# Two attentions on one core: images that hold each part once, key loads a slot ahead, small steps placed later

## The chip, the cores and the metric

The kernel runs on one core of a Trainium2 chip. The metric is the device time of one execution in microseconds, as the median of several runs. TensorE (PE in the profile) multiplies, VectorE (DVE) and ScalarE (ACT) work element by element and read TensorE's results from PSUM, GpSimd (POOL) works on SBUF only, and SyncE (SP) does nothing but send DMAs. Each engine runs its own instructions strictly in the order of the program; engines wait for one another, and for DMAs, by semaphores.

## The reference

```
x = A_x                                     # 2048 x 512, 32 heads of 16
g = sigmoid((x * gate_w).sum(-1))
A: q, k, v = x@wq, x@wk, x@wv, cut in 4 segments of 512 tokens; per segment
     a_dot = softmax(q k^T / 4 + causal mask) v
     a_mem = phi(q) M / (phi(q) z + 1e-6)          # M, z: sums over the segments before
     o = sigmoid(beta) * a_mem + (1 - sigmoid(beta)) * a_dot
   a = o @ wo
B: q, k, v = x @ wqkv;  b = softmax(q k^T / 4) v @ wob     # all 2048 keys
out = g * a + (1 - g) * b
```

A's `wq` and `wk` are scaled by 200, so the scores are large: each softmax needs its true row maximum, and queries and keys need more than one float32r pass. Each is therefore split in a high and a low part (`hi` = rounded to float32r, `lo` = the rest), and a score is hi·hi + hi·lo + lo·hi in one matmul of 48 contraction rows: 16 for each product. Two more rows, 48 and 49 of each half, hold minus the row maximum in two parts, so that the matmul of the scores subtracts it.

## The kernel before

**The projections** (the first 410 us or so) compute q, k and v of A and B from the transposed x, split q and k, and write them to HBM as *images* `QKD[kd, w, g]`: for each head rows of 2048 tokens. `kd` is A or B, `w` is 0 for queries and 1 for keys, `g` a group of eight heads. In A's images each part stands once (`lo`, `hi` for queries, `hi`, `lo` for keys); B's have three parts (`hi`, `lo`, `hi` and `hi`, `hi`, `lo`), and the third is written by a DMA on GpSimd's queue (L295). The same phase computes A's memory term and stores it to HBM (`OM`).

**The loop** has 32 slots, k = 0 to 31. A unit is four heads and 512 queries. Slot k handles unit 32+k, which is B's unit (`ub`), with 16 key tiles in 32 steps n = 0 to 31, and then unit k of A (`ua`) in five steps, n = 32 to 36. Two steps make one `it` (`it = n // 2`; the last step, 36, has it = 18). A step sends, in this order on TensorE: the transposed scores of two heads (`t_group`, L503), whose exponential ScalarE takes into `raw` (L509); the tasks that the plan puts there; and the product with V for an earlier step (`pv`, L525), summed in the PSUM bank `PVB`.

**Row maxima** are found a slot early, by tasks in the plan. `s_b` (L449) computes the scores of 128 queries against 512 keys for two heads into one of two PSUM buffers `sbk`, and VectorE reduces them (L451). B's unit 33+k has 32 such tasks: twelve in steps 20 to 31 of slot k-1, and twenty in steps 1 to 19 of slot k, step 1 having two. A's six tasks (`s_a`) are in steps 32 to 36 and step 0. At it = 10 `m_chain` (L460 to L470) makes minus the maximum in two parts, and after step 24 `m_rows` sends it into the query tile.

**The end of a unit.** `fin_copy` copies `PVB` to SBUF (L532 on VectorE for A, in step 0 of the next slot; L534 on ScalarE for B, in step 33) and writes it to HBM (L536). `fin_load` reads back the sums' row in another shape (L544) and the outputs (L542). `fin_rec` takes the reciprocal on VectorE (L549, then L553 for B or L551 for A) and writes it (L555). `fin_bc` reads it back, spread over the partitions (L561). Every second slot `fin_norm` multiplies on GpSimd (L565), fetches the memory term for B (L568), and for A adds the two branches (L570). `out_split` splits a block of 128 tokens for the output matmul: ScalarE rounds (L584), GpSimd subtracts (L585). `out_mm` (L591) multiplies it with `wo` and `wob` in step 20 of slots 9 and later. `beside(k, it)` says at which `it` each of these is put into the program.

**Loads.** `load_q` and `load_kb` (both L370) read query tiles and B's keys, all 2048 tokens of four heads. B's key buffers are three (`KB`, named `kb` and `xh` in the profile, since two of them are former x tiles), its query tiles three. In slot k after it = 2 the keys of index k+2 are loaded; the row maxima of that index begin at step 20 of the same slot. `load_q(ua+1)` and `load_ka` follow after it = 6, B's values (`load_vb`) and `wo` after it = 8.

**The order** is written out by hand: nothing reorders it. All these DMAs go through SP's one queue in program order; a DMA that has to wait for data holds all that follow. In the trace a key load of A waits 26 times (39.6 us in all) for the landing of a `d<-rd`, the eighth DMA before it in the queue, though it uses nothing of it.

Of the kernel before, what the change touches and what calls it, by code (L numbers as in the profile page):

```python
# [7 lines left out]
FT = mybir.dt.float32  # L8
# [10 lines left out]
E = 16  # L19
SEQ = 2048  # L20
DM = 512
C = 512
NC4 = SEQ // C
NT = SEQ // 128
# [3 lines left out]
S_FIRST = 10  # L28
S_LAST = 10
# [4 lines left out]
def gated_mix_kernel(ctx, tc, x, wq, wk, wv, wo, beta, wqkv, wob, gate_w, out):  # L34
    nc = tc.nc
# [6 lines left out]
    D = ctx.enter_context(tc.tile_pool(name="dram", bufs=1, space=DRAM))  # L42
# [52 lines left out]
    def misc():  # L95
        return bank(mode["misc"])

    QKD = {}
    for kd in "AB":
        for w in range(2):  # L100
            for g in range(4):
                QKD[kd, w, g] = D.tile([8, (3 if kd == "B" else 2) * E + 2 * (w == 0), SEQ], FT, name=f"d{kd}{w}{g}")
    VD = {kd: D.tile([SEQ, 4, 8, E + 1], FT, name=f"vd{kd}") for kd in "AB"}
    GD = D.tile([SEQ], FT, name="gd")
    OM = {}
# [168 lines left out]
    def qk_job(ws, kd, g, w, c):  # L274
        b = misc()
        n = 0
        for xi, wi in TERMS:
            for k in range(4):
                nc.tensor.matmul(b, WS[ws][w][wi][:, k, :], (XH, XL)[xi][c][:, k, :], start=n == 0, stop=n == 11)  # L279
                n += 1  # L280
        st = X.tile([128, 2, C], FR, name="st", bufs=4)
        phi = kd == "A" and (c > 0 if w == 0 else c < NC4 - 1)
        if phi:
            ph = PHI[g, w, c] = X.tile([128, C], FT, name=f"phi{w}")
            nc.vector.tensor_scalar(ph, b, 0.0, None, op0=OP.min)
        nc.scalar.activation(st[:, 0], b, AF.Copy)
        if phi:
            nc.scalar.activation(ph, ph, AF.Exp)
        nc.vector.tensor_tensor(st[:, 1], b, st[:, 0], op=OP.subtract)  # L289
        if phi:  # L290
            nc.vector.scalar_tensor_tensor(ph, b, 0.0, ph, op0=OP.max, op1=OP.add)
        img = QKD[kd, w, g][:, :, c * C:(c + 1) * C]
        for n, a in enumerate(((0, 1, 0), (0, 0, 1))[w] if kd == "B" else ((1, 0), (0, 1))[w]):
            eng = nc.gpsimd if n == 2 else nc.sync
            eng.dma_start(img[:, E * n:E * n + E], st[:, a].bitcast(FT))  # L295
        if w == 0 and c == 0:
            nc.sync.dma_start(QKD[kd, w, g][:, (3 if kd == "B" else 2) * E:].rearrange("h r (n t) -> h r n t", t=64),
                              aux[:, 1, None, :].to_broadcast([E, 2 * NT, 64]))


# [61 lines left out]
    def load_qk(dst, kd, w, qd, c):  # L362
        img = QKD[kd, w, qd // 2]
        v = img.rearrange("(q p j) r t -> q j r p t", q=2, p=2)
        cs = slice(c * C, (c + 1) * C) if c is not None else slice(0, SEQ)


        for d0, r0, n in ((0, 0, img.shape[1]),) if kd == "B" else ((0, 0, 16), (16, 0, 32)) if w else ((0, 0, 32), (32, 16, 18)):
            for j in range(2):
                nc.sync.dma_start(dst.bitcast(FT)[64 * j + d0:64 * j + d0 + n], v[qd % 2, j, r0:r0 + n, :, cs])  # L370

# [4 lines left out]
    def q_of(u):  # L376
        return QA[u % 2] if u < 32 else QB[u % 3]
# [4 lines left out]
    def load_q(u):  # L382
        kd, qd, c = UN[u]
        load_qk(q_of(u), kd, 0, qd, c)
# [5 lines left out]
    def load_kb(k, c=None):  # L390
        dst = KB[k % 3] if c is None else KB[k % 3][:, :, c * C:(c + 1) * C]
        load_qk(dst, "B", 1, k % 8, c)
# [6 lines left out]
    def load_vb(g):  # L399
        v_src(VB[g % 2], "B", g % 4, None)  # L400
# [145 lines left out]
    def fin_rec(u):  # L546
        kd, qd, c = UN[u]
        r = AT.pop(("r", u))
        nc.vector.reciprocal(r, r)  # L549
        if kd == "A":  # L550
            nc.vector.scalar_tensor_tensor(r, r, nq[:, qd:qd + 1], grow[:, 0, c], op0=OP.mult, op1=OP.mult)  # L551
        else:
            nc.vector.tensor_tensor(r, r, grow[:, 1, c], op=OP.mult)  # L553
        AT["rd", u] = D.tile([128, E], FT, name=f"rd{u}")
        nc.sync.dma_start(AT["rd", u], r)  # L555
# [7 lines left out]
    def fin_norm(kd, g, c):  # L563
        o, d = AT["o"][c % 2][:, g, int(kd == "B")], AT["d"][int(kd == "B")]
        nc.gpsimd.tensor_tensor(o, o, d, op=OP.mult)  # L565
        if kd == "B":
            if c:
                nc.sync.dma_start(d, OM[g, c])  # L568
        elif c:
            nc.gpsimd.tensor_tensor(o, o, AT["d"][1], op=OP.add)  # L570
# [12 lines left out]
    def out_split(c, t):  # L583
        nc.scalar.activation(AT["oh"], o_cols(c, t), AF.Copy)  # L584
        nc.gpsimd.tensor_tensor(AT["ol"], o_cols(c, t), AT["oh"], op=OP.subtract)  # L585
# [19 lines left out]
    def tail_split(t, gs, a, eng=None):  # L605
        oh, ol = [x[:, gs, a] for x in tail_ops(t)]
        o = o_cols(3, t)[:, gs, a]
        if eng:
            nc.scalar.copy(oh, o)
        else:  # L610
            nc.vector.tensor_copy(oh, o)
        (eng or nc.vector).tensor_tensor(ol, o, oh, op=OP.subtract)
# [20 lines left out]
    def todo(fn, *a):  # L633
        return lambda: fn(*a)
# [86 lines left out]
    for blk in range(16):  # L721
        g, c = divmod(blk, 4)
# [11 lines left out]
        n = blk + 1 + (c == 2)  # L734
# [90 lines left out]
    NG = 2 * NT + 5  # L825
# [34 lines left out]

    def beside(k, it):

        for f, it0, u in ((fin_load, NT + 1, 32 + k), (fin_rec, 1, 31 + k), (fin_bc, 2, 31 + k),
                          (fin_load, 1, k - 1), (fin_rec, 4, k - 1), (fin_bc, 5, k - 1)):
            if it == it0 and (k or it0 > NT):
                f(u)
        c, j = divmod(k - 1, 8)
        if k and j % 2:
            for kd, it0 in (("B", 4), ("A", 12)):
                if it == it0:  # L870
                    fin_norm(kd, j // 2, c)
        if k >= 8 and k % 2 == 0 and it == 14:
            out_split(k // 8 - 1, k // 2 % 4)
        if (k, it) == (31, 4):
            grest = AT["grest"] = AT["o"][0][64:, 0, 0]
            nc.sync.dma_start(grest, GD[3 * C:].rearrange("(o t) -> o t", o=1).to_broadcast([64, C]))
        if (k, it) == (31, 9):
            grest = AT["grest"]
            nc.vector.tensor_scalar(grest, grest, nh[64:, 3:4], None, op0=OP.mult)
        if (k, it) == (31, NT + 2):  # L880
            fin_rec(63)
        if k == 31 and it == 8:
            o = AT["o"][1][:64, 3, 0]
            nc.gpsimd.tensor_tensor(o, o, AT["d"][0][:64], op=OP.mult)
        if k == 31 and it < 8 and it % 2 == 0:
            for a in range(2):
                tail_split(it // 2, slice(0, 3), a)
# [9 lines left out]
    for k in range(31):  # L897
        if k:
            spread([todo(s_b, 33 + k, *t) for t in (sorted(ST_B, key=lambda t: t[2]) if k == 1 else ST_B)],
                   [(k - 1, n) for n in range(2 * S_FIRST, 2 * NT)] + [(k, n) for n in [1] + list(range(1, 2 * S_LAST))])  # L900
        else:
            spread(st33[EARLY:], sorted([(0, n) for n in range(2 * S_LAST)] + [(0, 2 * n) for n in range(4)]))
        for n, t in enumerate(ST_A):
            plan.setdefault((k, 2 * NT + n) if n < 5 else (k + 1, 0), []).append(todo(s_a, k + 1, *t))

    for k in range(32):
        ua, ub = k, 32 + k
        banks = T3 + [SBK[0][:, n] for n in range(2)] * (k == 31)
        for n in range(NG):
            it = n // 2 if n < NG - 1 else NT + 2  # L910
            t_group(*(ub, n) if n < 2 * NT else (ua, n - 2 * NT), banks)
            for f in plan.get((k, n), []) + ex[k][0].get(n, []):
                f()
            pvs(k, n)
            for f in ex[k][1].get(n, []):
                f()
            if n % 2 == 0 and n < NG - 1:
                continue
            beside(k, it)
            if it == S_LAST:  # L920
                m_chain(k + 1)
            if it == 4 and not k:
                late()
            if it == (2 if k else 4) and k < 30:
                load_q(ub + 2)
                for c in (None,) if k else range(NC4):
                    load_kb(k + 2, c)
            if it == 6 and k < 31:
                load_q(ua + 1)
                load_ka(ua + 1)  # L930
                if (ua + 1) % 2 == 0:
                    load_va(ua + 1)
            if it == 8:
                if k % 2 == 0 and k < 30:
                    load_vb(k // 2 + 1)
                if 1 <= k <= 4:
                    load_wo(k - 1)
# [16 lines left out]
    for t in range(4):  # L954
        d = den[:, t * 128:(t + 1) * 128]
# [37 lines left out]
```

## Time and profile before

| | us |
|---|---|
| median of 3 runs | 2071.38 |
| lowest, highest | 2065.68, 2074.39 |
| the profiled execution | 2075.72 |
| its span, first to last instruction | 2073.9 |
| granted TensorE clock, mean | 0.988 |

The profile is of one execution. Its rows give a start in us from the span's start, a duration, an engine, a line of the kernel and what is written from what; a bracket behind a row is the engine's idle time before it and what ended that. The names of the buffers stand without their numbers.

### The profile page before, as it was taken

Reading aid. Unit: us, or ns where it says so; the run is one execution under the profiler, and the core shown is the slowest. Engines: PE = TensorE matmul, PEld = TensorE weight load, DVE = VectorE, ACT = ScalarE, POOL = GpSimd, SP = SyncE. Lnnn points to the kernel's source line nnn. Section 1 sums busy time; section 2 is a strip of 40 time slices with the busy share of each in tenths; the row PEclk is TensorE's granted clock in tenths of the full one; section 3 lists DMA queues with packets and bytes.
Section 4 is the critical chain, followed back from the end, with each engine's and each line's share of the span. In section 5 each row is a group of like instructions: output and inputs, shape, how many; then the busy total and the mean of one; then the engine's idle time right before and its main releaser. Section 6 shows DMA issues by size and latency. Waiting matters only on the chain.

```text
span 2073.9 us, 43532 instructions
## 1 busy us (share of the span) xinstructions
PE 1977.6 (95%) x17517; PEld 958.7 (46%) x17517; DVE 1633.2 (79%) x1825; ACT 1432.9 (69%) x2703; POOL 276.1 (13%) x506
## 2 busy tenths in 40 slices
PE   7999898899999999999999999999999999999988
PEld 5777676533344343444444444444444444344434
DVE  6134564599999999898989898989888888888832
ACT  3232232388888888878787778787878777777783
POOL 2300010011111001111111111111111111101111
PEclk9999999899999999999999999999999999999999
DMA  6766566654544444343434443444444443444201
GB/s 209 178 175 189 176 194 172 185 125 107 119 100 108 94 108 101 82 108 82 108 82 109 82 108 82 105 85 102 89 94 95 88 103 79 100 87 98 60 30 52
DMA packets 165173, 230.88 MB, mean 111 GB/s; under 512 B 39644, under 2 KB 89836, under 8 KB 159212
## 3 DMA queue, kind: packets, MB, share of 16 engines
q1 hardware_dynamic: 157420, 211.69, 42.3%
q0 software_dynamic: 7552, 16.41, 3.5%
q8 instruction: 138, 2.26, 0.5%
q14 instruction: 63, 0.52, 0.1%
HBM read 148.21 MB, written 76.55 MB: 108 GB/s over the span
## 4 chain that ended last, share of the span: by engine, by line
PE 71%; DVE 10%; DMA 10%; ACT 4%; issue 2%; SPq 2%; POOL 0%; ACTq 0%; DVEq 0%; POOLq 0%
PE pvb L525 25%; PE tb L503 13%; PE sbk L449 9%; DVE mxb L451 7%; PE mb L503 6%; DMA xh<-dB 3%; ACT raw L509 2%; PE tb L591 2%; PE sbk L428 2%; PE tb L279 2%; DMA dA<-st 2%; DMA kb<-dB 1%; PE mb L279 1%; PE sbk L431 1%; PE mb L591 1%
## 5 line engine op out<-in xcount | busy, mean ns | idle before, releaser
L451 DVE TENSOR_REDUCE mxb<-sbk 128x2 f32<-128x1024 f32 x1024 | 1204.2, 1218 | 67.7 <-PE sbk L449 64.4
L509 ACT ACTIVATE raw<-tb 128x512 f32<-128x512 f32 x1557 | 885.8, 597 | 191.7 <-PE tb L503 93.2
L525 PE MATMUL pvb<-raw,vb 128*17 128x256 f32 (+1 forms) x8072 | 639.5, 389 | 0.0
L509 ACT ACTIVATE raw<-mb 128x512 f32<-128x512 f32 x780 | 465.6, 597 | 87.5 <-PE tb L503 61.1
L503 PE MATMUL tb<-qb,xh 64*128 64x512 f32 x880 | 333.6, 494 | 1.5 <-ACT raw L509 0.8
L449 PE MATMUL sbk<-xh,qb 64*128 64x512 f32 x1344 | 279.3, 402 | 28.3 <-DVE mxb L451 15.0
L525 PEld LDWEIGHTS pvb<-raw,vb 128*17 128x17 f32 x8072 | 134.4, 95 | 334.5 <-issue 327.5
L503 PE MATMUL mb<-qb,xh 64*128 64x512 f32 x437 | 215.9, 494 | 1.2 <-ACT raw L509 0.8
L512 POOL TENSOR_SCALAR_AFFINE_SELECT raw<-raw 128x256 f32<-128x256 f32 (+1 forms) x320 | 115.3, 361 | 748.0 <-ACT raw L509 739.9
L503 PEld LDWEIGHTS tb<-qb,xh 64*128 64x128 f32 x880 | 125.5, 183 | 189.6 <-issue 100.1
L503 PE MATMUL tb<-qb,kb 64*128 64x512 f32 x463 | 176.2, 496 | 2.6 <-DMA qb<-mr 1.1
L435 DVE TENSOR_REDUCE mx<-sbk 128x2 f32<-128x768 f32 (+1 forms) x128 | 139.8, 1092 | 44.2 <-PE sbk L431 35.3
L449 PE MATMUL sbk<-kb,qb 64*128 64x512 f32 x704 | 148.9, 409 | 13.3 <-DVE mxb L451 11.7
L449 PEld LDWEIGHTS sbk<-xh,qb 64*128 64x128 f32 x1344 | 135.3, 186 | 46.6 <-DVE mxb L451 32.1
L503 PEld LDWEIGHTS mb<-qb,xh 64*128 64x128 f32 x437 | 80.0, 183 | 90.0 <-issue 49.3
L503 PE MATMUL mb<-qb,kb 64*128 64x512 f32 x241 | 118.7, 492 | 0.7 <-DVE st L289 0.7
L503 PEld LDWEIGHTS tb<-qb,kb 64*128 64x128 f32 x463 | 65.9, 183 | 101.3 <-issue 50.7
L525 PE MATMUL pvb<-raw,va 128*17 128x256 f32 (+2 forms) x1280 | 94.8, 384 | 4.2 <-ACT pvs L534 0.8
L565 POOL TENSOR_TENSOR o<-o,d 128x512 f32<-128x512 f32 x31 | 39.8, 1282 | 410.8 <-DMA d<-rd 365.6
L437 DVE TENSOR_REDUCE mx<-sbk 128x4 f32<-128x1024 f32 x64 | 61.4, 960 | 37.6 <-PE sbk L431 37.6
L428 PE MATMUL sbk<-ka,qa 64*128 64x256 f32 (+3 forms) x512 | 85.9, 344 | 0.0
L449 PEld LDWEIGHTS sbk<-kb,qb 64*128 64x128 f32 x704 | 70.5, 186 | 30.2 <-DVE mxb L451 19.2
(266 smaller groups left out, 1866.4 us busy)
## 6 DMA issues: line engine op xcount, KB each, us to landing
xh<-dB SPq DMA_DIRECT2D x38, 768.0 KB
vb<-vdB SPq DMA_DIRECT2D x16, 1088.0 KB
kb<-dB SPq DMA_DIRECT2D x22, 768.0 KB
dB<-st SPq DMA_DIRECT2D x64, 256.0 KB
dA<-st SPq DMA_DIRECT2D x64, 256.0 KB
pd<-pvs SPq DMA_DIRECT2D x64, 256.0 KB
qb<-dB SPq DMA_DIRECT2D x64, 200.0 KB
dB<-st POOLq DMA_DIRECT2D x32, 256.0 KB, 7.3
```

The source lines that it names most:

```text
L279: nc.tensor.matmul(b, WS[ws][w][wi][:, k, :], (XH, XL)[xi][c][:, k, :], start=n == 0, stop=n == 11)
L428: nc.tensor.matmul(b[:, j, c0:c0 + n], q_of(u)[r, p, i * 128:(i + 1) * 128], k_of(u, p)[r, :n], start=True, stop=False)
L435: nc.vector.tensor_reduce(m[:, :, p, i], b[:, :, :n], axis=AX.X, op=OP.max)
L437: nc.vector.tensor_reduce(m[:, :, :, i], b.rearrange("q j (p k) -> q j p k", p=2)[:, :, :, :n], axis=AX.X, op=OP.max)
L449: nc.tensor.matmul(b[:, j], q_of(u)[r, p, i * 128:(i + 1) * 128], k_of(u, p)[r, kc * C:(kc + 1) * C], start=True, stop=True)
L451: nc.vector.tensor_reduce(MXB[u][:, :, p, i, kc], b, axis=AX.X, op=OP.max)
L503: nc.tensor.matmul(bs[j][:, c0:c0 + w], k_of(u, h // 2)[r, 128 * it:128 * it + 128], q_of(u)[r, h // 2, q0:], start=True, stop=True)
L509: nc.scalar.activation(pt, bs[j], AF.Exp, scale=SCALE)
L512: nc.gpsimd.affine_select(out=m, in_=m, pattern=[[1, 128]] if n < 2 else [[0, 2], [1, 128]], compare_op=OP.is_ge, fill=0.0, base=0, channe ...
L525: nc.tensor.matmul(PVB[32 * h:32 * h + E + 1, q0 + lo:q0 + hi], vt[:, it, 4 * q + h, :], pt[:, lo:hi], start=it == 0 and lo == 0, stop=it ...
L565: nc.gpsimd.tensor_tensor(o, o, d, op=OP.mult)
L591: nc.tensor.matmul(b, (AT["oh"], AT["ol"])[oi][:, g, a], (AT["wh"], AT["wl"])[wi][:, g, a], start=n == 0, stop=n == 11)
```

## The change

- B's images have two parts like A's. The third DMA of each of B's query and key jobs, on GpSimd's queue, is gone. `load_qk` reads both kinds as A's were read before: queries in pieces of 32 and 18 rows, keys in pieces of 16 and 32 rows, each for two halves of the partitions, so four DMAs in place of two.
- B's queries and keys of the slot after next are loaded at it = 16 (`NT`), the step after `fin_copy` of B, instead of at it = 2 one slot later. Slot 0 still loads index 2 in four chunks.
- `fin_rec` and `fin_bc` move from it = 1 and 2 to 5 and 6 for B, and from 4 and 5 to 6 and 7 for A. `fin_norm` moves from 4 to 9 for B and from 12 to 13 for A, `out_split` from 14 to 18, the loads of B's values and of `wo` from 8 to 9.
- Of the two maximum tasks in step 1 one goes to step 36 of the slot before.

```diff
-                QKD[kd, w, g] = D.tile([8, (3 if kd == "B" else 2) * E + 2 * (w == 0), SEQ], FT, name=f"d{kd}{w}{g}")
+                QKD[kd, w, g] = D.tile([8, 2 * E + 2 * (w == 0), SEQ], FT, name=f"d{kd}{w}{g}")
...
-        for n, a in enumerate(((0, 1, 0), (0, 0, 1))[w] if kd == "B" else ((1, 0), (0, 1))[w]):
-            eng = nc.gpsimd if n == 2 else nc.sync
-            eng.dma_start(img[:, E * n:E * n + E], st[:, a].bitcast(FT))
+        for a in range(2):
+            r = E * (a if w else 1 - a)
+            nc.sync.dma_start(img[:, r:r + E], st[:, a].bitcast(FT))
...
-        for d0, r0, n in ((0, 0, img.shape[1]),) if kd == "B" else ((0, 0, 16), (16, 0, 32)) if w else ((0, 0, 32), (32, 16, 18)):
+        for d0, r0, n in ((0, 0, 16), (16, 0, 32)) if w else ((0, 0, 32), (32, 16, 18)):
...
-        for f, it0, u in ((fin_load, NT + 1, 32 + k), (fin_rec, 1, 31 + k), (fin_bc, 2, 31 + k),
-                          (fin_load, 1, k - 1), (fin_rec, 4, k - 1), (fin_bc, 5, k - 1)):
+        for f, it0, u in ((fin_load, NT + 1, 32 + k), (fin_rec, 5, 31 + k), (fin_bc, 6, 31 + k),
+                          (fin_load, 1, k - 1), (fin_rec, 6, k - 1), (fin_bc, 7, k - 1)):
...
-            for kd, it0 in (("B", 4), ("A", 12)):
+            for kd, it0 in (("B", 9), ("A", 13)):
...
-        if k >= 8 and k % 2 == 0 and it == 14:
+        if k >= 8 and k % 2 == 0 and it == NT + 2:
             out_split(k // 8 - 1, k // 2 % 4)
...
-        if k == 31 and it == 8:
+        if k == 31 and it == 13:
             o = AT["o"][1][:64, 3, 0]
             nc.gpsimd.tensor_tensor(o, o, AT["d"][0][:64], op=OP.mult)
...
-                   [(k - 1, n) for n in range(2 * S_FIRST, 2 * NT)] + [(k, n) for n in [1] + list(range(1, 2 * S_LAST))])
+                   [(k - 1, n) for n in list(range(2 * S_FIRST, 2 * NT)) + [NG - 1]] + [(k, n) for n in range(1, 2 * S_LAST)])
...
-            if it == (2 if k else 4) and k < 30:
+            if it == 4 and not k:
                 load_q(ub + 2)
-                for c in (None,) if k else range(NC4):
-                    load_kb(k + 2, c)
+                for c in range(NC4):
+                    load_kb(2, c)
+            if it == NT and k < 29:
+                load_q(ub + 3)
+                load_kb(k + 3)
...
-            if it == 8:
+            if it == 9:
                 if k % 2 == 0 and k < 30:
                     load_vb(k // 2 + 1)
```

More of the change, by code (lines that the diff above doesn't have):

```diff
@@ L292, in qk_job @@
         img = QKD[kd, w, g][:, :, c * C:(c + 1) * C]
-        for n, a in enumerate(((0, 1, 0), (0, 0, 1))[w] if kd == "B" else ((1, 0), (0, 1))[w]):
-            eng = nc.gpsimd if n == 2 else nc.sync
-            eng.dma_start(img[:, E * n:E * n + E], st[:, a].bitcast(FT))
+        for a in range(2):
+            r = E * (a if w else 1 - a)
+            nc.sync.dma_start(img[:, r:r + E], st[:, a].bitcast(FT))
         if w == 0 and c == 0:
-            nc.sync.dma_start(QKD[kd, w, g][:, (3 if kd == "B" else 2) * E:].rearrange("h r (n t) -> h r n t", t=64),
+            nc.sync.dma_start(QKD[kd, w, g][:, 2 * E:].rearrange("h r (n t) -> h r n t", t=64),
                               aux[:, 1, None, :].to_broadcast([E, 2 * NT, 64]))
```

## The prediction

> **What bounds the kernel now.** I read the page first, then the busy time of single slots, then one quiet slot row by row. A slot runs from the first score matmul of B's step 0 to the next one.
>
> ```profile
> span 2073.9 us, 43532 instructions
> PE 1977.6 (95%) x17517; PEld 958.7 (46%) x17517; DVE 1633.2 (79%) x1825; ACT 1432.9 (69%) x2703; POOL 276.1 (13%) x506
> ```
>
> TensorE is busy for 95% of the span, so a loss must show as a longer slot. In the next view (columns: stretch, length, then busy time of each engine) the first line is the projections, the second a quiet slot, 23. The sums are of the eleven odd slots 9 to 29, the six even ones 10 to 20 and the four even ones 22 to 28.
>
> ```profile
> 0.00:412.00 412.00, 364.38 (x1699) 277.55 (x1700) 195.30 (x324) 121.52 (x251) 55.27 (x102) 0.95 0.65 185
> 1572.79:1623.83 51.04, 50.54 (x508) 21.61 (x504) 45.64 (x48) 41.27 (x77) 3.60 (x11) 1.00 0.39 83
> sum 564.95, PE 558.66 PEld 238.98 DVE 502.29 ACT 453.44 POOL 39.81; mean PE 50.79 PEld 21.73 DVE 45.66 ACT 41.22 POOL 3.62
> sum 317.15, PE 307.76 PEld 128.87 DVE 285.47 ACT 248.47 POOL 58.97; mean PE 51.29 PEld 21.48 DVE 47.58 ACT 41.41 POOL 9.83
> sum 216.38, PE 205.78 PEld 85.79 DVE 190.71 ACT 165.78 POOL 39.44; mean PE 51.45 PEld 21.45 DVE 47.68 ACT 41.44 POOL 9.86
> ```
>
> Quiet is 51.04 us; odd slots average 51.36, early even ones 52.86, late even ones 54.10. All even slots have about 2 us more VectorE time and 6 us more GpSimd time. Why VectorE's time counts shows in the quiet slot, which starts at 1572.79:
>
> ```profile
> 1575.00 4.61 DVE L451 TENSOR_REDUCE mxb<-sbk 128x2 f32<-128x1024 f32 x4
> ...
> 1586.96 0.23 DVE L551 SCALAR_TENSOR_TENSOR rec<-rec,nq,grow 128x16 f32<-128x16 f32 x1
> 1587.11 13.08 DVE L451 TENSOR_REDUCE mxb<-sbk 128x2 f32<-128x1024 f32 x11
> 1603.10 1.23 DVE L451 TENSOR_REDUCE mxb<-sbk 128x2 f32<-128x1024 f32 x1 [2.91 <-PE sbk L449]
> ...
> 1604.48 0.18 DVE L468 TENSOR_SCALAR mhi<-mx 128x32 fp32r<-128x32 f32 x1
> ```
>
> From 1575.0 VectorE runs 21 row maxima and two reciprocal pairs without a gap, 1.15 us a maximum where it has a backlog (4.61 / 4) and 1.19 over the last eleven; only the output matmuls (2.91 us) let it idle. TensorE can be two maxima ahead (two `sbk` buffers), so anything added here is soon paid by TensorE. The backlog comes from step 1, which holds two maximum tasks:
>
> ```profile
> 1575.44 0.50 PE L503 MATMUL mb<-qb,xh 64*128 64x512 f32 x1
> 1576.27 0.50 PE L449 MATMUL sbk<-kb,qb 64*128 64x512 f32 x2 [0.33 <-DVE mxb L451]
> ```
>
> In even slots GpSimd's products meet VectorE's small SBUF operations (timeline of slot 26, which starts at 1728.70, GpSimd's rows and VectorE's):
>
> ```profile
> 1761.70 1.28 POOL L565 TENSOR_TENSOR o<-o,d 128x512 f32<-128x512 f32 x1 [16.99 <-DMA ka<-dA]
> 1763.07 1.31 POOL L570 TENSOR_TENSOR o<-o,d 128x512 f32<-128x512 f32 x1
> ...
> 1761.74 1.28 DVE L468 TENSOR_SCALAR mhi<-mx 128x32 fp32r<-128x32 f32 x1
> ...
> 1763.15 1.27 DVE L470 SCALAR_TENSOR_TENSOR m<-mx,mhi 128x32 f32<-128x32 f32 x1
> ```
>
> The groups over the loop, with busy us and mean ns behind the bar:
>
> ```profile
> L551 DVE SCALAR_TENSOR_TENSOR rec<-rec,nq,grow 128x16 f32<-128x16 f32 x31 | 14.4, 465 | 1.1
> L470 DVE SCALAR_TENSOR_TENSOR m<-mx,mhi 128x32 f32<-128x32 f32 x32 | 12.4, 388 | 0.0
> L468 DVE TENSOR_SCALAR mhi<-mx 128x32 fp32r<-128x32 f32 x32 | 11.2, 349 | 1.1
> ```
>
> Each ends with the GpSimd operation it met: 1.28 us for 0.18. Over the loop that is (465-233) x 31 = 7.2 us in L551 and, with L468's quiet 0.18 for both, (388-180) x 32 = 6.7 in L470 and (349-180) x 32 = 5.4 in L468. The products are late because SP's queue stands behind the key load (SP's timeline, same slot):
>
> ```profile
> 1735.92 0.33 SPq L555 DMA_DIRECT2D rd<-rec  x1
> ...
> 1737.91 0.51 SPq L561 DMA_DIRECT2D d<-rd  x1
> 1738.47 0.87 SPq L370 DMA_DIRECT2D qb<-dB  x2
> 1739.39 0.81 SPq L370 DMA_DIRECT2D xh<-dB  x2
> 1743.14 0.34 SPq L555 DMA_DIRECT2D rd<-rec  x1
> ...
> 1755.67 0.53 SPq L561 DMA_DIRECT2D d<-rd  x1
> 1756.26 1.67 SPq L370 DMA_DIRECT2D qa<-dA  x4
> 1757.97 3.98 SPq L370 DMA_DIRECT2D ka<-dA  x4
> ...
> 1779.62 0.33 SPq L536 DMA_DIRECT2D pd<-pvs  x1
> ```
>
> The same load in the chain that ended last, and in TensorE's waits over the loop (total, times, longest):
>
> ```profile
> 1739.78 15.63 DMA xh<-dB
> ```
> ```profile
> PE sbk L449 <- DMA xh<-dB: 2.4, 3, 1.0
> ```
>
> A's reciprocals, sent at 1743.14, land only with the keys (15.63 us), so A's broadcast leaves at 1755.67 and its product starts at 1761.70, beside the maximum chain. The keys themselves are late in some slots; TensorE waits for them directly.
>
> **The change, part by part** (gains against the profiled execution, 2075.7 us: the span of 2073.9 and 1.8 around it).
>
> *Keys a slot ahead.* Every late key wait goes: the cover is now 24 steps instead of 15. Price: 4 x (54.10 - 52.86) + 11 x (51.36 - 51.04) = 8.5 us above; below, the 2.4 us of the row. I take 7, nearer the slots than the waits, since a wait also leaves VectorE idle.
>
> *B's reciprocal pair after step 11, A's after 13.* Now B's product, started by its broadcast, meets A's pair. Later B's product can start 2 us (1735.92 to 1737.91) and a broadcast's 5 us (row below) behind B's pair, at about +23 from the slot's start, and A's pair is done by +18.6 (below). L551 meets nothing: 7.2 us, less what the two buffers hide; I take 6 (0 to 7.2).
>
> *The maximum chain.* A broadcast takes 5.0 us from its issue to the product that waits for it, in slot 30, which loads no keys; a reciprocal row takes 3.75 from its issue to the reciprocal that waits (last slot; SP's rows and the waiting engine's):
>
> ```profile
> 1957.20 0.53 SPq L561 DMA_DIRECT2D d<-rd  x1
> ...
> 1962.20 1.28 POOL L565 TENSOR_TENSOR o<-o,d 128x512 f32<-128x512 f32 x1 [6.46 <-DMA d<-rd]
> ...
> 1997.36 0.51 SPq L544 DMA_DIRECT2D rec<-pd  x1
> ...
> 2001.11 0.25 DVE L549 RECIPROCAL rec<-rec 128x16 f32<-128x16 f32 x1 [2.92 <-DMA rec<-pd]
> ```
>
> From a slot's start: A's old pair ends at 1587.1 - 1572.8 = 14.3; four steps of 1.19 later, less the 0.3 saved at step 2 (next part), is 18.8. Its reciprocals are in HBM 2 us later, but now A's queries and keys (eight DMAs, 1.7 + 4.0 us by the rows) are issued ahead of its broadcast: 24 to 24.6, landing 5.0 later, product and sum (2.6 us) from 29 or 29.6 to 31.6 or 32.2. L468 stands at 1604.48 - 1572.79 = 31.7, then 0.3 earlier. So the end of the sum grazes it, 0.2 to 0.8 us in eleven slots instead of 1.1: of the 12.1 us in L468 and L470 I take back 7 (0 to 12.1). In slots 1 to 8, which have no output matmuls, the chain comes 2.9 us sooner and can now be hit; also `wo`'s GpSimd copies arrive earlier. I charge 2 us (0 to 5, four hits of 1.28).
>
> *One maximum task behind A.* The task's own matmuls cost as much in either step. What goes is the 0.33 of idle before step 2's maximum, and with it the backlog through which each reciprocal pair (about 0.4 us) bites later; against it, step 2's scores may wait for a bank anyway. I take 0.3 x 30 slots = 9 us; bounds 0 and, with a second hold of the same size, 0.6 x 30 = 18.
>
> *The split for the output at the slot's end.* ScalarE's 1.06 us goes from the stretch in which every step has two exponentials to the seam, where steps are longer. GpSimd's 2.38 us then lies beside the PVB copy L532 (one line's durations, min/median/max; the group of L585 with its mean).
>
> ```profile
> L584 ACT ACTIVATE oh<-o x12: 1057/1059/1059, 831.6 to 1981.3; 128x1024 fp32r<-128x1024 f32 x12
> L451 DVE TENSOR_REDUCE mxb<-sbk x64: 1207/1216/1227, 1679.6 to 1775.6; 128x2 f32<-128x1024 f32 x64
> L585 POOL TENSOR_TENSOR ol<-o,oh 128x1024 fp32r<-128x1024 f32 x12 | 28.6, 2380 | 129.2 <-ACT oh L584 129.2
> ```
>
> L451 reads PSUM and holds 1207 to 1227 ns through slot 26's products, so I let L532, a PSUM reader too, run free: gain 2 us, bounds 4 and, if it were held 1 us in 12 slots, -12. [...]
>
> *Images with each part once.* These go from the projections (the page's DMA issues: count, size, median us to landing):
>
> ```profile
> dB<-st POOLq DMA_DIRECT2D x32, 256.0 KB, 7.3
> ```
>
> They are 8.4 MB of 185 GB/s x 412 us = 76 MB. TensorE idles 412 - 364 = 48 us there, partly for DMAs; a ninth of half of it is 3 us (-3 to 8; below zero because the first key chunks now take four DMAs each). In a slot SP issues four DMAs more, 4 x 0.43 us; SP waits for landings for most of it, so nothing, and 1.7 us before the bound rows if that cover were gone.
>
> *What is queued behind the early keys.* Keys and queries now leave right after B's sums, 4.0 us before a slot's start (1779.62 against 1783.60) and 0.3 more with the moved task. A's sums are written at about +2.5, behind the keys on the same queue; SP waits for that, then asks for the reciprocal row. Keys: last issue at -4.3 + 8 x 0.4 = -1.1, less than 15.6 to land since no broadcast is ahead of them; I take +10.5 (9 to 13). B's read-backs lie between, an estimated 2 us: sums written +12.5, row asked +13.1, and 2001.11 - 1997.36 = 3.75 to come: +16.9. VectorE wants it at 18.8 - 0.4 = +18.4. Margin 1.5, spread about as large: I charge 0.1 x 29 = 3 us (0 to 38).
>
> Sum: 7 + 6 + 7 - 2 + 9 + 2 + 3 - 3 = 29; 2075.7 - 29 = 2046.7. The median of the runs, 2071.4, is 4.3 below the profiled execution, so a median could come out at 2042; I name 2045, between the two.
>
> **Rivals.** *1. Order is not time.* GpSimd's products are moved in the program, but nothing holds them to a step: they start when the broadcast lands. If it lands 1 us later than reckoned, product and sum sit on the chain as now: 7 us less, 2052. For: eight DMAs now stand before A's broadcast. Against: the key load no longer does.
>
> *2. The sums come late* (the other side). The keys' 15.6 us now lie before A's sums. Each microsecond that they land after +12.0 delays L549, and with it every maximum behind it: 29 us in all. From +13.1 the 32 us gained elsewhere are eaten; at +13.9 the price is 55 and the time 2045 - 3 + 55 = 2097. For: 15.63 from the last issue would be +14.5. Against: the broadcast that is ahead of the keys now is gone. [...]
>
> *3. TensorE and ScalarE are the bound.* If step 2 waits for its score bank anyway, the moved task nets nothing, L551's 6 become 2 and the split's 2 nothing. 15 us less: 2060. For: TensorE is busy 50.54 of 51.04 us in the quiet slot. Against: the 0.33 gap is VectorE's.
>
> **How the numbers follow.** Forecast 0.48; rivals 1, 2, 3: 0.20, 0.17, 0.15. Half a per cent (10 us) is what a measurement of this kernel can tell. Faster: 0.48 + 0.20 + 0.06 of rival 3 = 0.74; same: the rest of 3 and 0.05 of 2 = 0.14; slower 0.12. The forecast's own range is 2034 to 2056; for 8 in 10, with most of the second rival left outside, 2030 to 2075.
>
> **What would show it.** Right: no wait of L449 for `xh` or `kb` in the loop; L551 at 0.23; L468 and L470 near 0.18 in most even slots; no 0.33 gap at step 2; a quiet slot of 50.7. Wrong: an idle L549 waiting for `rec<-pd`; quiet slots still at 51.0; L532 above 0.7 us in slots after an even one; products on the chain again.

## The result, and the profile after

| | before | after |
|---|---|---|
| median, us | 2072.89 (2065.68 to 2080.96, 4 runs) | 2010.82 (2007.75 to 2014.98, 4 runs) |
| ratio, 95% interval | | 0.9701 (0.9660 to 0.9742) |
| span of the profiled execution | 2073.9 | 2006.0 |
| first score matmul of the loop | 390.66 | 352.03 |
| slot 0 | 62.59 | 64.49 |
| slots 1 to 30 together | 1538.6 | 1507.7 |
| slot 31 and the output's tail | 82.1 | 81.8 |

The change gains 62 us by the medians, 67.9 between the two profiled executions. The forecast was 2045, its range 2030 to 2075: the direction was right, but it held less than half of the gain. Of the 67.9 us, 30.9 lie in slots 1 to 30, close to the 26 that the prediction's loop terms give (29 less the 3 for the images). 38.6 lie ahead of the loop, where 3 were expected.

The lines behind the changed places have moved up by one: L449 is L448, L468 and L470 are L467 and L469, L551 is L550, L532 is L531.

The busy time of two stretches of the changed kernel: the projections up to the first score matmul of the loop, and slot 23.

```profile
0.00:352.03 352.03, 334.63 (x1585) 259.45 (x1585) 180.44 (x310) 111.69 (x234) 36.19 (x71) 0.99 0.64 186
1515.48:1566.46 50.98, 50.59 (x508) 21.50 (x505) 45.94 (x49) 41.65 (x78) 5.98 (x11) 1.00 0.43 84
```

The first of them in the kernel before:

```profile
0.00:390.66 390.66, 344.42 (x1586) 265.64 (x1586) 180.52 (x310) 112.24 (x234) 52.88 (x98) 0.94 0.65 186
```

Two things are shorter. TensorE's idle time fell from 390.66 - 344.42 = 46.2 to 17.4 us. And the same matmuls are busy for 9.8 us less, at a granted clock (the third column from the right, 1.00 is full speed) of 0.99 instead of 0.94. The rate in the last column is the same, 186 GB/s.

The groups of the changed kernel from 400 to 1990 us (busy us and mean ns behind the bar):

```profile
L550 DVE SCALAR_TENSOR_TENSOR rec<-rec,nq,grow 128x16 f32<-128x16 f32 x31 | 7.3, 234 | 1.1
L467 DVE TENSOR_SCALAR mhi<-mx 128x32 fp32r<-128x32 f32 x31 | 10.0, 321 | 1.1
L469 DVE SCALAR_TENSOR_TENSOR m<-mx,mhi 128x32 f32<-128x32 f32 x31 | 6.8, 220 | 0.0
L531 DVE COPY pvs<-pvb 128x512 f32<-128x512 f32 x31 | 21.1, 681 | 0.0
```

The chain's two in the kernel before, over the same stretch:

```profile
L470 DVE SCALAR_TENSOR_TENSOR m<-mx,mhi 128x32 f32<-128x32 f32 x31 | 12.2, 395 | 0.0
L468 DVE TENSOR_SCALAR mhi<-mx 128x32 fp32r<-128x32 f32 x31 | 11.0, 354 | 1.1
```

And the longest of TensorE's waits from 352 to 1924 us of the changed kernel (total us, times, longest):

```profile
PE tb L502 <- ACT raw L508: 6.5, 23, 0.3
PE sbk L448 <- DVE mxb L450: 3.9, 6, 1.3
```

The reciprocal pair meets GpSimd no more (234 ns, it was 465). The two operations of the maximum chain fell from 354 and 395 ns to 321 and 220. TensorE waits for no key in the loop. The copy L531 takes its 0.68 us in every slot, also where GpSimd's 2.37 us of the output split lie beside it (slot 21, GpSimd's row and VectorE's):

```profile
1414.05 2.37 POOL L584 TENSOR_TENSOR ol<-o,oh 128x1024 fp32r<-128x1024 f32 x1 [0.55 <-ACT oh L583]
1415.30 0.68 DVE L531 COPY pvs<-pvb 128x512 f32<-128x512 f32 x1
```

### The profile page after: what moved, and what is told of

It is laid out like the page before. It is cut to its first block, busy times and chain, and to the rows that moved or that the text cites. A ratio compares the mean times of both kernels' runs of the same rounds, so it can differ in the third digit from the quotient of the medians.

```text
span 2006.0 us, 43688 instructions
## 1 busy us (share of the span) xinstructions
PE 1956.3 (98%) x17517; PEld 949.0 (47%) x17517; DVE 1631.9 (81%) x1825; ACT 1435.1 (72%) x2703; POOL 256.6 (13%) x474
## 4 chain that ended last, share of the span: by engine, by line
PE 89%; DMA 3%; DVE 3%; ACT 2%; SPq 2%; issue 1%; POOL 0%; ACTq 0%; POOLq 0%; DVEq 0%
PE pvb L524 31%; PE tb L502 17%; PE sbk L448 12%; PE mb L502 8%; PE tb L279 3%; PE sbk L427 2%; PE tb L590 2%; PE mb L279 2%; ACT raw L508 2%; PE pvb L279 2%; DVE mxb L450 2%; PE sbk L430 2%; PE mb L590 1%; PE sbk L279 1%; PE tb L262 1%
## 5 line engine op out<-in xcount | busy, mean ns | idle before, releaser
L450 DVE TENSOR_REDUCE mxb<-sbk 128x2 f32<-128x1024 f32 x1024 | 1222.7, 1222 | 49.4 <-PE sbk L448 45.7
L448 PE MATMUL sbk<-xh,qb 64*128 64x512 f32 x1344 | 287.6, 400 | 4.4 <-DVE mxb L450 3.3
L448 PE MATMUL sbk<-kb,qb 64*128 64x512 f32 x704 | 152.9, 408 | 0.8 <-DVE mxb L450 0.7
L448 PEld LDWEIGHTS sbk<-xh,qb 64*128 64x128 f32 x1344 | 138.8, 186 | 10.8 <-DVE mxb L450 7.0
L502 PE MATMUL tb<-qa,ka 64*128 64x384 f32 (+3 forms) x340 | 79.5, 372 | 0.0
L448 PEld LDWEIGHTS sbk<-kb,qb 64*128 64x128 f32 x704 | 72.1, 185 | 12.6 <-issue 6.5
```

What stands on the lines that cost most here:

```text
L448: nc.tensor.matmul(b[:, j], q_of(u)[r, p, i * 128:(i + 1) * 128], k_of(u, p)[r, kc * C:(kc + 1) * C], start=True, stop=True)
L450: nc.vector.tensor_reduce(MXB[u][:, :, p, i, kc], b, axis=AX.X, op=OP.max)
L502: nc.tensor.matmul(bs[j][:, c0:c0 + w], k_of(u, h // 2)[r, 128 * it:128 * it + 128], q_of(u)[r, h // 2, q0:], start=True, stop=True)
```

## Experiments

Beside times, each run gives the start of the first score matmul of the loop ("loop at") and the length of slots 1 to 30 ("loop"). The loop starts at 351.4 to 357.0 in seven runs with images of two parts and no extra write, at 383.0 to 393.0 in four with three; their means are 354 and 390. A single start lies up to 7 us from its mean, so it is sure to some 3 to 7 us.

### Which edit shortens the projections

**e1**: the kernel before, the images alone changed. **e2**: the changed kernel, the images alone as before.

```diff
 e1, against before
-                QKD[kd, w, g] = D.tile([8, (3 if kd == "B" else 2) * E + 2 * (w == 0), SEQ], FT, name=f"d{kd}{w}{g}")
+                QKD[kd, w, g] = D.tile([8, 2 * E + 2 * (w == 0), SEQ], FT, name=f"d{kd}{w}{g}")
...
+        for a in range(2):
+            r = E * (a if w else 1 - a)
+            nc.sync.dma_start(img[:, r:r + E], st[:, a].bitcast(FT))
...
+        for d0, r0, n in ((0, 0, 16), (16, 0, 32)) if w else ((0, 0, 32), (32, 16, 18)):
 e2, against after: the same lines the other way round
```

> The kernel before with nothing changed but the images: two parts, two writes a job, four DMAs a load. The prediction's term for this part was 3 us (-3 to 8): by it the time is about 2069 and the first loop step starts near 388. The reading of the two traces, in which the first loop step comes 38.6 us sooner, gives about 2035 and a first loop step near 352. If 352 appears here without the time following, the loop with the old order takes the gain back.

> The changed kernel with the images of three parts again (third part written on GpSimd's queue, two DMAs a load), all the other edits kept. If the images carry the projections' gain: first loop step near 390, about 2048. If an edit in the loop's order carries it (the key loads, the late steps): first loop step near 352, about 2011.

| | median, us | ratio to before | loop at | loop |
|---|---|---|---|---|
| e1 | 2180.4 | 1.0496 (1.0457 to 1.0534) | 354.4 | 1683.4 |
| e2 | 2041.9 | 0.9832 (0.9802 to 0.9862) | 392.4 | 1502.4 |

The images shorten the projections, and nothing else does: about 36 us (390 against 354). e1's expectation allowed that the old order of the loop takes this gain back; it took four times as much: e1 is 105 us slower than the kernel before, its loop 145 us longer. Its slot 17 in a row of the busy times, and in TensorE's rows at step 20:

```profile
1303.26:1360.75 57.49, 53.85 (x508) 23.54 (x504) 45.64 (x48) 41.26 (x77) 3.64 (x11) 0.94 0.40 74
```
```profile
1332.27 0.99 PE L449 MATMUL sbk<-xh,qb 64*128 64x512 f32 x2 [3.15 <-DMA xh<-dB]
```

The same slot of the kernel before:

```profile
1259.05:1310.29 51.24, 50.76 (x508) 21.85 (x504) 45.63 (x48) 41.24 (x77) 3.73 (x11) 1.00 0.39 83
```

SP's queue shows why the key is late. First e1, then before, both from +8.8 us of slot 17:

```profile
1312.10 0.51 SPq L561 DMA_DIRECT2D d<-rd  x1
1312.66 1.67 SPq L370 DMA_DIRECT2D qb<-dB  x4
1314.37 4.81 SPq L370 DMA_DIRECT2D xh<-dB  x4
...
1332.38 0.54 SPq L561 DMA_DIRECT2D d<-rd  x1
```
```profile
1267.89 0.51 SPq L561 DMA_DIRECT2D d<-rd  x1
1268.45 0.87 SPq L370 DMA_DIRECT2D qb<-dB  x2
1269.37 0.80 SPq L370 DMA_DIRECT2D xh<-dB  x2
...
1284.13 0.53 SPq L561 DMA_DIRECT2D d<-rd  x1
```

Eight DMAs are out 6.5 us after the first, four are out after 1.7 us; by the landings in the trace the last piece of the keys arrives at +28.9 in e1 and at +24.9 before. Step 20 asks at +25.9 in e1. Part of the delay is SP's own wait for the broadcast that it sent just ahead of these loads; in this slot of e1, and not in that of the kernel before, SP's waits have

```profile
SPq L370 <- DMA d<-rd: 2.8, 1, 2.8
```

The wait of 3.15 us made the slot 6.25 us longer: the other 3.1 us are TensorE's own busy time, 53.85 against 50.76, at a granted clock of 0.94 instead of 1.00. The clock fell during the wait, at 1331.92, and stayed at half for 6.83 us:

```profile
1331.92:1338.75 6.83, 6.48 (x18) 4.46 (x22) 1.23 (x1) 0.03 (x1) 0.00 (x0) 0.50 0.52 134
```

### Bytes, a held buffer, or GpSimd's queue

All of these are the changed kernel plus one write for each of B's query and key jobs, where the third part was written. `gw` is a tile that is loaded once; `X3` are rows that nobody reads.

```diff
+            nc.gpsimd.dma_start(X3[w, g][:, :, c * C:(c + 1) * C], gw)                        # e3, 256 KB
+            nc.gpsimd.dma_start(X3[w, g][0, :1, c * C:(c + 1) * C], st[:1, w].bitcast(FT))    # e4, 2 KB
+            nc.sync.dma_start(X3[w, g][:, :, c * C:(c + 1) * C], gw)                          # e5, 256 KB
+            nc.gpsimd.dma_start(X3[w, g][:, :, c * C:c * C + 16], gw[:, :16])                 # e6, 8 KB
+            for n in range(2):                                                                # e13, 512 KB
+                nc.gpsimd.dma_start(X3[w, g, n][:, :, c * C:(c + 1) * C], gw)
```

> The changed kernel with an extra write of 256 KB on GpSimd's queue where the third part was written, from a tile that is never rewritten into rows that nobody reads: the bytes and GpSimd's issue are back, but no buffer is held and GpSimd waits for no split. Theory 'traffic' (8.4 MB delay every other transfer of the projections): first loop step back to 385 to 390, about 2045. Theory 'hold' (GpSimd waits in program order for a split, and the split's buffer stays taken until the write has landed): 352 and 2011 as in the changed kernel.

> The changed kernel with a write of 2 KB (one row) of the split's part on GpSimd's queue where the third part was written: GpSimd waits for the split again and the buffer is held until the write has landed, but there are no bytes to speak of. Theory 'hold': first loop step back to 380 to 390, about 2045. Theory 'traffic': 352 and 2011.

> As e3 (the changed kernel, 256 KB of extra writes a job of B from a tile that is never rewritten into rows that nobody reads), but sent by SyncE's queue instead of GpSimd's. If the bytes cost the 25 us of e3: first loop step near 377 again, about 2030. If it is that they go through GpSimd's software queue: 352 to 357, 2011 to 2016.

> As e3 on GpSimd's queue, with the same 128 pieces a write but 64 bytes each instead of 2048 (8 KB a job). If the bytes cost the 25 us: first loop step 352 to 355, 2011 to 2015. If GpSimd's work on 128 pieces a write, or their number, does: near 377, about 2030.

> As e3, with two such extra writes a job of B on GpSimd's queue (16.8 MB instead of 8.4). If the projections are bound by bytes at a fixed rate: 16.8 MB at 186 GB/s is 90 us, first loop step near 440, 2100. If each 8.4 MB costs the 25 us of e3: near 403, 2060. If the queues had room left beyond what e3 took: less than 390.

| | extra MB, queue | median, us | ratio to before | loop at |
|---|---|---|---|---|
| after | 0 | 2010.8 | 0.9701 (0.9660 to 0.9742) | 352.0 |
| e4 | 0.07, GpSimd, buffer held | 2013.4 | 0.9704 (0.9679 to 0.9729) | 357.3 |
| e6 | 0.26, GpSimd | 2010.0 | 0.9695 (0.9672 to 0.9718) | 353.2 |
| e3 | 8.4, GpSimd | 2030.6 | 0.9780 (0.9756 to 0.9805) | 377.6 |
| e5 | 8.4, SyncE | 2039.3 | 0.9833 (0.9807 to 0.9858) | 383.4 |
| e13 | 16.8, GpSimd | 2051.7 | 0.9910 (0.9882 to 0.9939) | 398.8 |

In the main it is the bytes. The same 128 pieces with few bytes (e6) cost nothing. A buffer held with GpSimd waiting (e4) costs no more than starts differ. 8.4 MB cost 24 to 29 us against the mean start of 354, whichever queue sends them, and the next 8.4 MB another 21. That is 2.5 to 3.5 us a megabyte; at the projections' mean rate 8.4 MB would be 45 us, so a third to a half is hidden. Neither end that e13 named came true (440, or under 390); 403 is near. What is left of the 36, some 7 to 12 us, is not settled: it may be that a held buffer costs only while large writes are under way, which was not tried alone.

The projections of e13 in a row, and what its DMAs moved up to 398.80 (packets, MB, rate), as against after:

```profile
DMA packets 51842, 82.41 MB, mean 207 GB/s; under 512 B 12654, under 2 KB 21438, under 8 KB 51627
```
```profile
DMA packets 46701, 65.59 MB, mean 186 GB/s; under 512 B 11630, under 2 KB 20414, under 8 KB 46486
```

186 GB/s was not the most that the chip could move: with more to move it moved 207. The 16 DMA engines are busy for 0.64 to 0.68 of these stretches. What grows with the bytes are a few waits for transfers. Before and after, in TensorE's waits of the projections:

```profile
PE sbk L449 <- DMA xh<-dB: 10.0, 1, 10.0
PE mb L168 <- DMA raw<-in_A_x_dram: 5.7, 2, 3.3
PE sbk L449 <- DVE mxb L451: 5.3, 1, 5.3
PE sbk L350 <- DMA vm<-vdA: 4.7, 1, 4.7
```
```profile
PE sbk L350 <- DMA vm<-vdA: 3.3, 1, 3.3
PE mb L168 <- DMA raw<-in_A_x_dram: 2.5, 1, 2.5
...
PE sbk L448 <- DMA xh<-dB: 0.7, 1, 0.7
```

ScalarE, which waited 30.5 us for `dA<-st` to land before it could use a split's buffer again, waits for none after; this is its row before:

```profile
ACT st L286 <- DMA dA<-st: 30.5, 6, 9.0
```

### Keys, reciprocals and the moved task, each by itself

**e7** is e2 with the keys loaded after it = 2 again, **e9** the changed kernel with them there, **e10** the changed kernel with the reciprocals at their old places, **e12** the kernel before with only the reciprocals and products moved, **e8** the changed kernel with the task back in step 1.

```diff
 e7, e9
...
-            if it == NT and k < 29:
-                load_q(ub + 3)
-                load_kb(k + 3)
...
+            if it == (2 if k else 4) and k < 30:
+                load_q(ub + 2)
+                for c in (None,) if k else range(NC4):
+                    load_kb(k + 2, c)
 e12, against before (e10, against after: the other way round)
-        ... (fin_rec, 1, 31 + k), (fin_bc, 2, 31 + k), ... (fin_rec, 4, k - 1), (fin_bc, 5, k - 1)
+        ... (fin_rec, 5, 31 + k), (fin_bc, 6, 31 + k), ... (fin_rec, 6, k - 1), (fin_bc, 7, k - 1)
-            for kd, it0 in (("B", 4), ("A", 12)):
+            for kd, it0 in (("B", 9), ("A", 13)):
 e8, against after
-    list(range(2 * S_FIRST, 2 * NT)) + [NG - 1]] + [(k, n) for n in range(1, 2 * S_LAST)]
+    range(2 * S_FIRST, 2 * NT)] + [(k, n) for n in [1] + list(range(1, 2 * S_LAST))]
```

> The kernel of e2 (images of three parts, all other edits) with B's queries and keys loaded after it = 2 of the slot before their use again. By the prediction's term for the keys a slot ahead (7 us, 2.4 to 8.5) the time is 2049, 2044 to 2051. If with the keys late the other steps lose as well (a wait of TensorE also lowers the granted clock, as in e1), above 2060.

> The changed kernel (images of two parts) with B's queries and keys loaded after it = 2 again. If the load a slot ahead is worth what the prediction gave it: 2018 (7 us). If, as e7 against e2, nothing hangs on it once the reciprocals are late: 2011. If four DMAs a load need the longer cover (in e1 the last key piece landed 19.5 us after the first query DMA was issued, which from +5.6 is +25, where step 20 wants it): TensorE waits for keys of 0 to 3 us a slot and a lower clock, 2015 to 2100.

> The changed kernel with fin_rec, fin_bc and fin_norm at their old places (it = 1, 2, 4, 5 and 4, 12), the keys still a slot ahead. In the changed kernel the sums of B land at +12.3 and those of A at +17.1 from a slot's start, behind the keys; the old places want them at +6.7 and +13.9. If VectorE stands still for them and two score buffers cannot hide it: 3 to 6 us in each of 29 slots, 2100 to 2190. If it is hidden: 2011 plus at most the 29 us that the late steps bring, 2040.

> The kernel before with nothing changed but the places of fin_rec, fin_bc and fin_norm (it = 5, 6, 6, 7 and 9, 13); images of three parts, keys after it = 2, both maximum tasks in step 1, the split at it = 14. By the prediction's terms for L551, the maximum chain and its collisions (6 + 7 - 2 = 11): 2063. With the term for the keys as well, which here leave with no broadcast ahead of them (7): 2056. By the runs (the loop of e7 gains 37.7 us, of which the moved task is 8.8 by e8 and the split some 2): 27 us, 2047.

> The changed kernel with the maximum task of step 36 back in step 1. By the prediction's term (9 us): 2020. By the trace of the changed kernel, whose quiet slot is 0.12 us shorter and in which step 2 still shows 0.28 of idle, now behind ScalarE: 2014 to 2015.

| | median, us | ratio to before | loop at | loop |
|---|---|---|---|---|
| e7 | 2042.2 | 0.9841 (0.9809 to 0.9874) | 383.0 | 1500.9 |
| e9 | 2012.9 | 0.9712 (0.9682 to 0.9742) | 351.4 | 1507.3 |
| e10 | 2247.9 | 1.0830 (1.0797 to 1.0864) | 352.9 | 1746.7 |
| e12 | 2055.1 | 0.9910 (0.9876 to 0.9945) | 393.0 | 1518.0 |
| e8 | 2020.1 | 0.9745 (0.9719 to 0.9772) | 357.0 | 1516.5 |

The keys a slot ahead bring nothing: the loop is 1500.9 without and 1502.4 with them (e7, e2), 1507.3 and 1507.7 with the new images (e9, after). Once the reciprocals are late, no broadcast stands ahead of the keys: in slot 23 of e9 they are issued from +5.9 on instead of +9.4, and the last piece lands at +22.6, in time. By the landings of slots 2 to 28 the last piece comes at +25.4 on the mean in the kernel before, at +20.5 in e12, where only the reciprocals are late, and at +23.2 in e9, never after +25.3.

The late reciprocals carry the loop. Alone they gain 20.6 us in it (e12), where the expectation by the runs had 27. Taken out of the changed kernel, with the keys still early, they cost 239 us (e10), more than the 180 at most that its expectation allowed. There VectorE stands still for the sums that land behind the keys. Its rows in slot 23 of e10, and its waits over the loop:

```profile
1704.14 3.56 DVE L450 TENSOR_REDUCE mxb<-sbk 128x2 f32<-128x1024 f32 x3
1714.78 0.25 DVE L548 RECIPROCAL rec<-rec 128x16 f32<-128x16 f32 x1 [7.08 <-DMA pd<-pvs]
```
```profile
DVE rec L548 <- DMA rec<-pd: 156.0, 24, 8.3
...
DVE rec L548 <- DMA pd<-pvs: 32.6, 5, 7.1
```

189 us of VectorE's waits became 239 us of loop; the mean granted clock of the whole execution is 0.943 (after 0.995).

The moved task is worth 1516.5 - 1507.7 = 8.8 us, 0.29 a slot, as the prediction had it. The second reading in e8's expectation was wrong. It compared quiet slots of before and after, 51.04 and 50.92, and took the difference for the task's; but the images cost 0.2 us in each slot (next part), and in e2, without them, an odd slot is 50.76 on the mean and mostly 50.73.

### What the images cost in the loop

The loop of e2 is 5.3 us shorter than that of the changed kernel. The two run alike up to step 20, the first task that reads the new keys. After and e2, the weight loader's instructions there (durations in ns, first and last start):

```profile
L448 PEldq EVENT_SEMAPHORE  x4: 51/51/51, 1540.2 to 1540.6; - x4
```
```profile
L448 PEldq EVENT_SEMAPHORE  x2: 51/51/51, 1577.7 to 1577.9; - x2
```

Each tile comes in four DMAs instead of two. The first matmul pair that reads it has two more waits to carry, and TensorE's next matmul starts 0.21 us later against the slot's start: at 1541.11 and 1578.37 in slots that start at 1515.48 and 1552.95, so +25.63 against +25.42. TensorE, busy for 50.59 of the slot's 50.98 us, does not make this up, and it costs 0.18 us in each of 30 slots. That the loss begins at this pair is shown, in e9 against e7 too; the two waits themselves take 0.1 us, and what the other 0.1 us is stays open.

### The collisions that remained

**e11** and **e14** put A's loads behind A's broadcast.

```diff
-            if it == 6 and k < 31:
+            if it == 8 and k < 31:      # e11;  it == 10 in e14
                 load_q(ua + 1)
                 load_ka(ua + 1)
```

> The changed kernel with A's query, key and value loads after it = 8 instead of 6, so behind A's broadcast on the queue. The product and the sum of A on GpSimd then come some 2 us sooner and leave the maximum chain alone in all even slots: even slots fall from a mean of 51.30 to that of odd ones, 50.96, over ten slots 3.4 us, 2007. If the broadcast does not land sooner, or A's keys come late to the maxima of step 32: 2011 or more.

> The changed kernel with A's query, key and value loads after it = 10, behind A's broadcast and behind the fetch of the memory term that fin_norm of B sends at it = 9. In e11 A's product was off the chain, but the sum still waited for the memory term, which came behind the keys, and met the maximum chain in slots 10 to 20. If that was the last collision: sum at +28 to +30, even slots at 51.0 as the odd ones, loop 1504 instead of 1507.7, 2007. If A's keys then come late to the maxima of step 32 (+43): slower than 2011.

| | median, us | ratio to before | loop at | loop | even slots 10 to 28, mean |
|---|---|---|---|---|---|
| after | 2010.8 | 0.9701 (0.9660 to 0.9742) | 352.0 | 1507.7 | 51.30 |
| e11 | 2010.2 | 0.9690 (0.9665 to 0.9715) | 356.5 | 1507.5 | 51.34 |
| e14 | 2008.3 | 0.9678 (0.9653 to 0.9704) | 353.6 | 1505.7 | 51.07 |

In the changed kernel GpSimd's product and sum still met the chain, slot 26, GpSimd and VectorE:

```profile
1699.48 1.28 POOL L564 TENSOR_TENSOR o<-o,d 128x512 f32<-128x512 f32 x1 [4.97 <-DMA d<-rd]
1700.84 1.32 POOL L569 TENSOR_TENSOR o<-o,d 128x512 f32<-128x512 f32 x1
```
```profile
1700.04 0.76 DVE L467 TENSOR_SCALAR mhi<-mx 128x32 fp32r<-128x32 f32 x1
...
1700.92 1.28 DVE L469 SCALAR_TENSOR_TENSOR m<-mx,mhi 128x32 f32<-128x32 f32 x1
```

e11 moved the product away, but the sum then waited for the memory term, which is fetched behind the keys, and hit the chain in slots 10 to 16. In e14 both are clear; the groups over its loop:

```profile
L467 DVE TENSOR_SCALAR mhi<-mx 128x32 fp32r<-128x32 f32 x31 | 6.3, 203 | 1.1
L469 DVE SCALAR_TENSOR_TENSOR m<-mx,mhi 128x32 f32<-128x32 f32 x31 | 5.7, 184 | 0.0
```

That the collisions lengthen the chain is shown (321 and 220 ns on the mean in the changed kernel, 203 and 184 here); the 2 us that the loop gains are less than its time can be told from that of the changed kernel.

## Why the prediction was right and wrong

| step of the prediction | forecast, us | measured, us | by |
|---|---|---|---|
| images, in the projections | 3 | 36 to 39 | e1, e2; before against after |
| images, in the loop | 0 | -5.3 | after against e2 |
| keys a slot ahead | 7 | 0 (-1.5) | e2 against e7; e9 |
| pair later, chain, new collisions | 6 + 7 - 2 | 20.6 | e12 |
| one task behind A | 9 | 8.8 | e8 |
| split at the slot's end | 2 | 8.3 | e7 less e12 and e8, by difference |
| sums late | -3 | 0 | no such wait after |
| slot 0 | none | -1.9 | before against after |

With 38.6 in the first row, -1.5 for the keys and 0.2 in the tail the right column gives 67.8 us, the difference of the spans within rounding. Since one row is a difference of the others, this is no check of the single rows.

The loop's sum came near, 30.9 us for 26, partly by luck: the split brought 6.3 us more than its term and the sums cost 3 less, and against that stands the 5.3 us of the images, which were put at nothing.

**The step that failed** is "Images with each part once", and in it the sentence "TensorE idles 412 - 364 = 48 us there, partly for DMAs; a ninth of half of it is 3 us". It priced the bytes as their share of TensorE's idle time (46 of the 48 us lie ahead of the loop, which starts at 390.66), and took TensorE's busy time as fixed. Neither holds: the idle time fell by 28.8 us for a tenth fewer bytes (72.6 to 65.6 MB), since much of it stood at a few places where a transfer was late (the rows with DMA above add up to 20.4 us before and to 6.5 after); and 9.8 us came out of the busy time, with the clock. The same sentence's 8.4 MB and 185 GB/s, divided, give 45 us. That was the upper bound that the range should have reached to, and "-3 to 8" did not. The runs showed 36 to 39 us in its place, of which the bytes alone brought 24 to 29 (e3, e5); the cause of the remaining 7 to 12 is open.

The same part of the prediction took four more DMAs a slot as "nothing", since it looked at SP's time to issue them. They cost 5.3 us over the loop at their reader, TensorE, and with the old order of the loop 145 (e1).

**Keys a slot ahead**: mis-sized, and put down to the wrong edit. The slots that the prediction used (54.10 against 52.86) were slow since the keys stood behind a broadcast, and it is the late reciprocal that removes the broadcast. By its terms the late steps and the keys make 18 together; e12 measured 20.6 for the late steps alone, which include what the keys gain by them.

**B's reciprocal pair after step 11**: right, 234 ns as forecast. **The maximum chain**: the product grazes it as forecast; of 12.1 us, 31 x (354 - 321 + 395 - 220) ns = 6.4 came back where 7 were expected.

**One maximum task**: right, 0.29 a slot for 0.3. The gap before step 2's maximum, 0.34 us behind VectorE in e8, is gone as forecast, though a gap of 0.28 behind ScalarE now stands one matmul earlier. The gain comes there: in slot 23 step 3's scores start 0.6 us sooner after the slot's start than in e8, and 0.3 of it is given back in step 36, where the task now stands. The quiet slot, forecast at 50.7, is 50.92; without the new images it is 50.73 (e2).

**What is queued behind the early keys**: right nearly to the number. Forecast for the last key +10.5, for A's sums +16.9. The landings in the trace of slot 23 are +10.8 and +17.2, and VectorE asks at +18.2. Rival 2 therefore had its margin of 1 us, and e10 shows what lies behind it. The keys' four pieces a tile hardly lengthen the transfer: counted from the first query DMA the last key lands 14.7 us later in four pieces (after) and 14.4 in two (e2); on the mean of slots 2 to 28 it is 14.8 and 14.7. In e9 against e7 the last key does land 2.5 us later by that count (17.5 and 15.0), but its DMA is also issued 3.5 us later, so the delay is SP's and not the transfer's.

**Rival 1** happened in seven of eleven even slots (10, 12 and 22 to 30), where the product or the sum still met the chain. **Rival 3** did not: the moved task brought its 9 us.

**The split**: it has no run of its own. The 8.3 is a difference, so it also holds what e7's edits do together and the loads that went from it = 8 to 9, and it is the least sure of the rows. L531 was not held (0.68 us beside GpSimd's 2.37 in slot 21, 681 ns on the mean), as the prediction chose.

## What to carry to other kernels

Price a transfer's bytes in a phase with many DMAs between two ends: nothing, and bytes over the phase's own rate; an idle share of the engines is no argument for the lower one (here some 3 us a megabyte, with the DMA engines busy for 0.65). Before an edit of a queue is given a gain, ask which of the edits removes what stands in front: here a later reciprocal did what the earlier load was taken to do, while the earlier load without it cost 12% (e10 against after). An edit that splits a transfer must be priced at its reader too: here two more waits ahead of TensorE's weight loads came with 0.18 us a slot (after against e2).

## What the hardware showed that was not expected

- A wait of TensorE cost more than itself: 3.15 us of waiting made a slot 6.25 us longer, its granted clock 0.94 instead of 1.00 (slot 17 of e1); over the projections the clock is 0.94 with 46 us idle (before) and 0.99 with 17 (after).
  Shorter waits were followed by half the clock too, but not all of them: after 2.00 us of waiting until 352.03 in the changed kernel it is 0.50 from 352.41 to 355.82, and after 1.69 us until 280.13 in the kernel before 0.50 from 280.13 to 283.54, while a wait of 1.85 us, until 1765.61 in slot 26 of the kernel before, left it at 1.00.
- A semaphore wait ahead of a weight load took 51 ns; with two more of them TensorE's next matmul started 0.2 us later (after against e2).
- The projections' DMA rate is 186 GB/s with 65.6 and with 72.6 MB (after, before), but 207 with 82.4 (e13): an even rate was no sign of a limit.
